# Keys and values of two heads on alternate partitions, and a new order of VectorE's steps, in a decode kernel fed from memory

## The chip, the cores and the metric

The kernel runs on one core of a Trainium2 chip. A core has a matrix engine (TensorE, in the profile PE, and PEld for its weight loads), a vector engine (VectorE, DVE), a scalar engine (ScalarE, ACT), GpSimd (POOL) and a queue engine that issues most loads (SyncE, SP). Sixteen DMA engines move data between the chip's memory (HBM) and the core's buffer (SBUF); TensorE writes into PSUM.

The metric is the device time of one execution in microseconds (us). Before the change the median of three runs is 128.31 us (128.28 to 128.5).

## The reference

Two branches read the same normalized row of 576 numbers, and both are added to it. Branch A is attention of one query over the last 4096 keys of a cache, with 32 query heads and 16 key heads, so that two query heads share a key head. Branch B is a gated MLP with a spatial gate, which for a sequence of length one is a scale and a shift.

```python
def _A_ref(x, k_cache, v_cache, wq, wo):
    W = min(4096, max(256, Sk // 4))          # 4096 of 65536
    q = (x @ wq).reshape(B, Sq, 32, 128)
    k = repeat(k_cache[:, :, Sk - W:, :], 2)   # 16 key heads for 32 query heads
    v = repeat(v_cache[:, :, Sk - W:, :], 2)
    scores = einsum('bhqd,bhkd->bhqk', q, k) * 128 ** (-0.5)
    p = softmax(scores)
    return einsum('bhqk,bhkd->bhqd', p, v).reshape(B, Sq, 4096) @ wo

def _B_ref(x, w_in, w_sp, b_sp, w_out):
    z = gelu(x @ w_in)                         # 4608 wide
    z1, z2 = z[..., :2304], layernorm(z[..., 2304:])
    g = w_sp * z2 + b_sp                       # one number each
    return (z1 * g) @ w_out

xn = layernorm(x)
return x + _A_ref(xn, ...) + _B_ref(xn, ...)
```

Weights, keys and values are bf16. Every byte of them is used once, and together they are 50.96 MB.

## The kernel before

**Loads.** All large loads go through one queue (SP), in the order in which lines 96 to 109 write them: `wq` in two parts, key pairs k0 and k1, `win` in three parts, then k2, v0, k3, v1 and so on to v7, then `wout` and `wo` in six parts (10, 8, 6, 4, 2 and 2 of its 32 rows a partition). They share a ring of seven slots of 20.7 KB a partition (`RING`). A load is issued when the transfer queue's turn comes and the slot that it takes has been given back by the last instruction that read it; SP waits in order, so a load that must wait holds up the ones after it.

**Keys and values.** One load brings two heads (`load_kv`, line 86). Each partition gets 32 consecutive positions of the first head (8 KB) and 32 of the second.

**Scores.** TensorE needs the 128 elements of a key along partitions. DVE transposes blocks of 32 by 32 words of four bytes (`t_head`, line 243: two instructions of 128x1024 a head); `s_head` (line 251) then multiplies with `Qb`, in which each query is laid out so that four accumulating matmuls per 512 positions give the scores of both query heads. The four heads of a group (GK) use four sets of 32 PSUM partitions of `S`; two such tiles alternate between groups.

**Softmax.** `sm_a` (line 275) takes the maximum over a partition's 1024 scores, spreads it over the partitions of a head with small transposes (`spread`, line 263) and lets ACT compute the exponential of the whole tile, with the sum. `sm_b` (line 286) transposes the result (`pt`, one instruction), spreads the sums the same way, takes the reciprocal, and lets ACT copy sixteen blocks of 32x32 words into `PT`.

**Product with the values.** `pv` (line 302) runs 128 matmuls into the one tile `ops`, 32 for each head of the group. `yb` (line 313) multiplies with the reciprocals and a mask (`om`), adds up (`on`), gathers with four small matmuls (`yps`) and copies to `Y`.

**MLP.** `z_mms` (line 330) multiplies with `win`; `z_rest` and `z_norm` (lines 340 and 363) are gelu, the second layernorm and the gate, in small steps on DVE with one exponential on ACT and one power on POOL.

**Order.** The order is written out by hand (line 70 turns the planner's own order off), and each engine works through its instructions in that order. The loop from line 381 runs over the 16 heads; `sm_a` of a group stands after the transposes of the first head of the next one, `sm_b` after those of the second, `yb` a group later, `pv` after the fourth. After the loop come the last group's softmax, `yb` of the third group, `pv`, two thirds of the product with `wout` (`out_hv`), `yb` of the last group, the rest of `wout` and the 64 matmuls with `wo`. These accumulate in two PSUM tiles; two copies and one store end the kernel.

Of the kernel before, what the change touches and what calls it, by code (L numbers as in the profile page):

```python
# [16 lines left out]
HKV = 16  # L17
DH = 128
# [2 lines left out]
F = 4608  # L21
FH = 2304
NT = W // 128
TB = 8
NB = NT // TB
GK = 4
NG = HKV // GK
NR = 98
NF = FH // 128
CW = D // 2  # L30
# [9 lines left out]
def kernel(  # L40
# [34 lines left out]
    def ring_tile(name, rows, width):  # L75
        t = ring.tile([P, SLOT], BF16, name=name, tag="ring")
        return t[:, 0:rows * width].rearrange("p (s c) -> p s c", c=width)
# [6 lines left out]
        return [(lo + s, v[:, s, :]) for s in range(n)]  # L84

    def load_kv(src, m, name):
        v = ring_tile(f"{name}{m}", 2, NT * DH)
        nc.sync.dma_start(v, src[0, 2 * m:2 * m + 2, SK - W:SK, :].rearrange("h (p t) d -> p h (t d)", p=P))
        return {2 * m + h: v[:, h, :].rearrange("p (t d) -> p t d", d=DH) for h in range(2)}

    def load_n(src, per, lo, n, name):
        v = ring_tile(f"{name}{lo}", n, D)
# [3 lines left out]
    K, V = {}, {}  # L96
    wq_sb = load_halves(A_wq, 0, 5, "wq") + load_halves(A_wq, 5, 4, "wq")
    for m in range(2):
        K.update(load_kv(A_k_cache, m, "k"))
    win_sb = sum((load_halves(B_w_in, lo, 3, "win") for lo in (0, 3, 6)), [])  # L100
    for m in range(2, HKV // 2):
        K.update(load_kv(A_k_cache, m, "k"))
        V.update(load_kv(A_v_cache, m - 2, "v"))
    for m in range(HKV // 2 - 2, HKV // 2):
        V.update(load_kv(A_v_cache, m, "v"))
    wout_sb = load_n(B_w_out, NF, 0, NF, "wout")
    wo_sb = []
    for n in (10, 8, 6, 4, 2, 2):
# [34 lines left out]
    idv = ident[:].rearrange("p (i c h) -> p i c h", i=4, h=2)[:, :, 0:4, :]  # L143
    cm = const.tile([P, 4], FP32, name="cm")
    nc.vector.tensor_reduce(out=cm[:], in_=idv.rearrange("p i c h -> p c i h"), op=ALU.add,
                            axis=mybir.AxisListType.XY)
    dmask = const.tile([P, 4, DH], FP32, name="dmask")
    nc.gpsimd.tensor_copy(dmask[:], cm[:].unsqueeze(2).to_broadcast([P, 4, DH]))
    ihm = const.tile([P, 4, 2], FP32, name="ihm")
    nc.vector.reduce_sum(ihm[:], idv.rearrange("p i c h -> p i h c"), axis=AXX)  # L150

    sel = const.tile([P, 4, 32], FP32, name="sel")
    nc.gpsimd.memset(sel[:], 0.0)
    selv = sel[:].rearrange("p q (i h e) -> p q i h e", i=4, h=2)
    for dq in range(4):
        nc.gpsimd.tensor_copy(selv[:, dq, :, :, dq], ihm[:])
    S = []
    for n in range(2):
        t = ps_s.tile([P, 2, 512], FP32, name=f"S{n}")
# [4 lines left out]

    mx = lead.tile([P, 32], FP32, name="mx")
    nc.gpsimd.memset(mx[:], 0.0)
    lx = const.tile([P, 32], FP32, name="lx")
    nc.gpsimd.memset(lx[:], 1.0)
    mb = const.tile([P, 32], FP32, name="mb")
    nc.gpsimd.memset(mb[:], 0.0)  # L170
    lb = const.tile([P, 32], FP32, name="lb")
    nc.gpsimd.memset(lb[:], 1.0)


    nc.tensor.matmul(ps_x[:, 0:NS], lhsT=rmat[:], rhs=x64[:], start=True, stop=True)  # L175
# [64 lines left out]
    KT = {}  # L240
    st = {}

    def t_head(j):
        kT = ktpool.tile([P, NT, 2, 32, 2], BF16, name=f"kT{j}", tag="kT")
        src = K[j].rearrange("p t d -> p (t d)").bitcast(FP32)
        dst = kT[:].rearrange("p t b k e -> p (t b k e)").bitcast(FP32)
        for hf in range(2):
            nc.vector.transpose(dst[:, 1024 * hf:1024 * (hf + 1)], src[:, 1024 * hf:1024 * (hf + 1)])  # L248
        KT[j] = kT

    def s_head(j):
        g, i = divmod(j, GK)
        kv = KT.pop(j)[:].rearrange("p t b k e -> p b e t k")
        for hf in range(2):
            for be in range(4):
                nc.tensor.matmul(  # L256
                    S[g % 2][32 * i:32 * i + 8, hf, :],
                    lhsT=Qb[:, j, be].rearrange("p a h -> p (a h)"),
                    rhs=kv[:, be // 2, be % 2, 16 * hf:16 * hf + 16, :],
                    start=(be == 0), stop=(be == 3), tile_position=(0, 32 * i),  # L260
                )

# [12 lines left out]
    def sm_a(g):  # L275
        s = S[g % 2]
        nc.vector.tensor_reduce(out=mx[:, 0:1], in_=s[:], op=ALU.max, axis=mybir.AxisListType.XY)  # L277
        bk = spread(mx, mb, g, ALU.max, "m")
        nm = work.tile([P, 1], FP32, name=f"nm{g}", tag="nm")
        nc.vector.tensor_scalar_mul(nm[:], bk[:, 0:1], -SCALE)  # L280
        p = work.tile([P, 1024], BF16, name=f"p{g}", tag="p")
        nc.scalar.activation(p[:], s[:].rearrange("p a n -> p (a n)"), ACT.Exp, bias=nm[:, 0:1], scale=SCALE,  # L282
                             accum_out=lx[:, 0:1])
        st[g] = {"p": p}

    def sm_b(g):
        d = st[g]
        pt = work.tile([P, NT, 32], BF16, name=f"pt{g}", tag="pt")
        nc.vector.transpose(pt[:].rearrange("p t x -> p (t x)"), d["p"][:])  # L289
        lbk = spread(lx, lb, g, ALU.add, "l")  # L290
        rs = work.tile([P, 1], FP32, name=f"rs{g}", tag="rs")
        nc.vector.reciprocal(rs[:], lbk[:, 0:1])
        PT = work.tile([P, GK, NT, 2], BF16, name=f"PT{g}", tag="PT")
        pt4 = pt[:].rearrange("p t x -> p (t x)").bitcast(FP32).rearrange("p (t x) -> p t x", x=16)
        PT4 = PT[:].rearrange("p i t h -> p (i t h)").bitcast(FP32).rearrange("p (i t) -> p i t", i=GK)
        for i in range(GK):
            for a in range(4):
                nc.scalar.copy(PT4[32 * a:32 * a + 32, i, :], pt4[32 * i:32 * i + 32, :, a])  # L298
        d["PT"] = PT
        d["rs"] = rs  # L300

    def pv(g):
        d = st[g]
        for tb in range(NT // 4):
            for i in range(GK):
                nc.tensor.matmul(  # L306
                    ops[32 * i:32 * i + 8, :],
                    lhsT=d["PT"][:, i, 4 * tb:4 * tb + 4, :].rearrange("p t h -> p (t h)"),
                    rhs=V[GK * g + i][:, 4 * tb:4 * tb + 4, :],
                    start=(tb == 0), stop=(tb == NT // 4 - 1), tile_position=(0, 32 * i),  # L310
                )

    def yb(g):
        d = st[g]
        om = work.tile([P, 4, DH], FP32, name=f"om{g}", tag="om")
        nc.vector.scalar_tensor_tensor(out=om[:].rearrange("p c d -> p (c d)"), in0=ops[:],  # L316
                                       scalar=d["rs"][:, 0:1], in1=dmask[:].rearrange("p c d -> p (c d)"),
                                       op0=ALU.mult, op1=ALU.mult)
        on = work.tile([P, DH], FP32, name=f"on{g}", tag="on")
        nc.vector.reduce_sum(on[:], om[:].rearrange("p c d -> p d c"), axis=AXX)  # L320
        yps = ps_m.tile([P, 32], FP32, name=f"yps{g}", tag="m")
        for dq in range(4):
            nc.tensor.matmul(  # L323
                yps[32 * g:32 * g + 32, :], lhsT=sel[:, dq, :], rhs=on[:, 32 * dq:32 * dq + 32],
                start=(dq == 0), stop=(dq == 3), tile_position=(0, 32 * g),
            )
        nc.vector.tensor_copy(Y[32 * g:32 * g + 32, :], yps[32 * g:32 * g + 32, :])


    def z_mms():  # L330
# [6 lines left out]
                                 skip_group_check=True)  # L337
        return zps

    def z_rest(zps):  # L340
# [6 lines left out]
        nc.vector.tensor_mul(u[:], u[:], z[:])  # L347
        th = const.tile([P, 2, NF], FP32, name="th")
        nc.scalar.activation(th[:], u[:], ACT.Exp, scale=-2.0 * GELU_C)
        nc.vector.tensor_scalar_add(th[:], th[:], 1.0)  # L350
        nc.vector.reciprocal(th[:], th[:])
        G = const.tile([P, 2, NF], FP32, name="G")
# [25 lines left out]
        nc.vector.tensor_mul(hv[:], G[:, 0], zn[:])  # L378
        return hv

    for j in range(HKV):
        t_head(j)
        g, o = divmod(j, GK)
        if g > 0 and o == 0:
            sm_a(g - 1)
        if g > 0 and o == 1:
            sm_b(g - 1)
        s_head(j)
        if j == GK - 1:
            zps = z_mms()  # L390
        if j == GK + 1:
            G, sz = z_rest(zps)

            acc = []
            for n, pool in enumerate((ps_a, ps_b)):
                t = pool.tile([P, 512], FP32, name=f"acc{n}", tag="ab"[n])
                acc.append(t[32 * n:32 * n + 1, 0:CW])
                nc.tensor.matmul(acc[n], lhsT=ones_b[:, 0:1], rhs=xrow[:, CW * n:CW * (n + 1)],
                                 start=True, stop=False, tile_position=(0, 32 * n))
        if j == GK + 2:  # L400
            hv = z_norm(G, sz)
        if g > 1 and o == 0:
            yb(g - 2)
        if g > 0 and o == 3:
            pv(g - 1)

    def out_mms(lhs, col, wv, last):
        for n in range(2):
# [15 lines left out]
    out_hv(2)  # L424
    for t, wv in wo_sb:
        out_mms(Y, t, wv, t == 31)
# [35 lines left out]
```

## Time and profile before

| | |
|---|---|
| median of 3 runs | 128.31 us (128.28 to 128.5) |
| profiled execution | 128.45 us, its span 126.6 us |
| PE, PEld | 76.2 and 33.7 us busy (60% and 27%) |
| DVE | 74.0 us busy (58%), 155 instructions |
| ACT, POOL | 23.3 and 3.6 us busy |
| read from HBM | 50.96 MB, 403 GB/s over the span |
| key transposes on DVE | 32 of 1213 ns |
| score matmuls on PE | 128, 43.4 us busy |
| exponentials on ACT | 4 of 1113 ns |
| copies to `PT` on ACT | 64 of 241 ns |
| granted TensorE clock, mean | 0.771 |

The profile is one execution. The span goes from its first to its last instruction; the other 1.85 us of the execution's time lie around it. The page cuts the span into 40 slices of 3.2 us and gives for each how busy an engine was, in tenths, and what the DMA engines moved. Groups of instructions are named by line, engine, operation and tile (`kT<-k`), with the number of partitions by elements. The chain follows back from the last instruction to what released each step. "Idle before" is time in which an engine waited just before an instruction, with what ended the wait. Busy times of matmuls overlap, since TensorE runs them in a pipeline and on several column groups at a time.

### The profile page before, as it was taken

To read this page: it belongs to the slowest core of one execution; us is meant where nothing else is said; L and a number is where in the kernel's file an instruction comes from. 1 tells how busy PE (TensorE), PEld (TensorE's weight loads), DVE (VectorE), ACT (ScalarE), POOL (GpSimd) and SP (SyncE) were. 2 spreads that over 40 slices of the span, in tenths; PEclk is the share of its full clock that TensorE was granted. 3 is DMA by queue.
4 is the path that set the end of the run, shared out by engine and by line. 5 is a ranking of instruction groups with operands and counts; after the bars stand their busy time and mean duration, and the time that the engine had idled before them with its cause. 6 is when DMAs were issued, how large, how long until landed. Compare 5 with 4: busy or idle time off the path is not lost.

```text
span 126.6 us, 1582 instructions
## 1 busy us (share of the span) xinstructions
PE 76.2 (60%) x610; PEld 33.7 (27%) x610; DVE 74.0 (58%) x155; ACT 23.3 (18%) x77; POOL 3.6 (3%) x19
## 2 busy tenths in 40 slices
PE   0002831399999797508449555993579920798461
PEld 0001301132699721102113121331113300345230
DVE  6704135999100499454299889998899359123001
ACT  1200011000000003930000306503065037500001
POOL 3401000000000000000100000000000000000000
PEclk9999998559995555875556995599655798559999
DMA  4999999999999999999999999999999999999950
GB/s 136 447 402 425 407 432 427 440 433 441 419 411 427 422 422 430 427 427 427 430 427 430 427 427 425 425 430 422 430 430 422 432 460 443 405 412 422 412 219 0
DMA packets 6174, 51.04 MB, mean 403 GB/s; under 512 B 534, under 2 KB 536, under 8 KB 1048
## 3 DMA queue, kind: packets, MB, share of 16 engines
q1 hardware_dynamic: 6082, 50.96, 95.5%
q8 instruction: 4, 0.07, 0.2%
q10 hardware_dynamic: 86, 0.00, 0.0%
q14 instruction: 2, 0.02, 0.0%
HBM read 50.96 MB, written 0.00 MB: 403 GB/s over the span
## 4 chain that ended last, share of the span: by engine, by line
issue 41%; DVE 25%; DMA 15%; PE 12%; ACT 4%; POOLq 0%; POOL 0%; ACTq 0%
DVE kT L248 11%; DMA wo<-in_A_wo_dram 8%; PE S L256 7%; DMA x<-in_A_x_dram 7%; ACT PT L298 3%; PE ops L306 3%; DVE mx L277 3%; DVE pt L289 3%; DVE on L320 2%; DVE om L316 1%; ACT p L282 1%; PE yps L323 1%; DVE mt L266 1%; DVE mb L272 1%; PE ps_x L185 0%
## 5 line engine op out<-in xcount | busy, mean ns | idle before, releaser
L256 PE MATMUL S<-kT,Qb 128*8 128x512 bf16 x128 | 43.4, 532 | 19.6 <-DVE kT L248 19.2
L248 DVE STREAM_TRANSPOSE kT<-k 128x1024 f32<-128x1024 f32 x32 | 37.0, 1213 | 10.7 <-DMA k<-in_A_k_cache_dram 10.6
L256 PEld LDWEIGHTS <-Qb 128*8 128x8 bf16 x128 | 12.5, 104 | 45.6 <-issue 39.2
L298 ACT COPY PT<-pt 32x32 f32<-32x32 f32 x64 | 15.4, 241 | 13.5 <-DVE pt L289 12.7
L282 ACT ACTIVATE p<-S,nm 128x1024 bf16<-128x1024 f32 x4 | 4.5, 1113 | 55.5 <-DVE nm L280 55.5
L306 PE MATMUL ops<-v,PT 128*8 128x512 bf16 x128 | 14.3, 478 | 0.4 <-ACT PT L298 0.4
L335 PEld LDWEIGHTS <-win 128*128 128x128 bf16 x162 | 10.1, 163 | 0.4 <-issue 0.4
L335 PE MATMUL zps<-XT,win 128*128 128x2 bf16 x162 | 10.2, 202 | 0.0
L323 PE MATMUL yps<-on,sel 128*32 128x32 f32 x32 | 1.9, 209 | 9.6 <-DVE on L320 9.6
L409 PE MATMUL acc<-wo,Y 128*1 128x288 bf16 x64 | 4.9, 285 | 3.2 <-DMA wo<-in_A_wo_dram 3.0
L277 DVE TENSOR_REDUCE mx<-S 128x1 f32<-128x1024 f32 x4 | 4.8, 1205 | 2.4 <-PE S L256 2.4
L175 PE MATMUL ps_x<-x,rmat 64*128 64x9 bf16 x1 | 0.2, 163 | 9.4 <-DMA x<-in_A_x_dram 9.4
L306 PEld LDWEIGHTS <-PT 128*8 128x8 bf16 x128 | 4.1, 91 | 6.3 <-issue 3.0
L289 DVE STREAM_TRANSPOSE pt<-p 128x1024 bf16<-128x1024 bf16 x4 | 4.8, 1210 | 1.4 <-ACT p L282 1.4
L316 DVE SCALAR_TENSOR_TENSOR om<-ops,rs,dmask 128x512 f32<-128x512 f32 x4 | 3.0, 742 | 4.2 <-PE ops L306 4.2
L429 DVE CAST res<-acc 1x288 bf16<-1x288 f32 x1 | 0.4, 446 | 8.5 <-PE acc L409 8.5
L323 PEld LDWEIGHTS yps<-on,sel 128*32 128x32 f32 x32 | 1.5, 122 | 11.5 <-DVE on L320 9.6
L208 PE MATMUL qps<-wq,XT 128*2 128x512 bf16 x36 | 4.0, 627 | 0.8 <-DVE XT L199 0.8
L320 DVE TENSOR_REDUCE on<-om 128x128 f32<-128x512 f32 x4 | 4.1, 1026 | 0.1
L409 PEld LDWEIGHTS <-Y 128*1 128x1 bf16 x64 | 2.8, 82 | 5.3 <-issue 4.4
L219 DVE CAST q_rep<-qps 128x512 bf16<-128x512 f32 x2 | 1.4, 692 | 4.6 <-PE qps L208 3.9
L217 ACT CAST q_rep<-qps 128x512 bf16<-128x512 f32 x2 | 1.2, 586 | 14.6 <-DVE q_rep L219 14.6
(89 smaller groups left out, 37.7 us busy)
## 6 DMA issues: line engine op xcount, KB each, us to landing
k<-in_A_k_cache_dram SPq DMA_DIRECT2D x8, 2048.0 KB, 23.3
v<-in_A_v_cache_dram SPq DMA_DIRECT2D x8, 2048.0 KB, 20.7
win<-in_B_w_in_dram SPq DMA_DIRECT2D x3, 1728.0 KB, 22.4
wout<-in_B_w_out_dram SPq DMA_DIRECT2D x1, 2592.0 KB, 26.6
wq<-in_A_wq_dram SPq DMA_DIRECT2D x1, 2560.0 KB, 8.7
wq<-in_A_wq_dram SPq DMA_DIRECT2D x1, 2048.0 KB, 12.9
wo<-in_A_wo_dram SPq DMA_DIRECT2D x1, 1440.0 KB
wo<-in_A_wo_dram SPq DMA_DIRECT2D x1, 1152.0 KB
```

Source lines behind the costliest of these rows:

```text
L248: nc.vector.transpose(dst[:, 1024 * hf:1024 * (hf + 1)], src[:, 1024 * hf:1024 * (hf + 1)])
L256: nc.tensor.matmul(S[g % 2][32 * i:32 * i + 8, hf, :], lhsT=Qb[:, j, be].rearrange("p a h -> p (a h)"), rhs=kv[:, be // 2, be % 2, 16 * hf ...
L277: nc.vector.tensor_reduce(out=mx[:, 0:1], in_=s[:], op=ALU.max, axis=mybir.AxisListType.XY)
L282: nc.scalar.activation(p[:], s[:].rearrange("p a n -> p (a n)"), ACT.Exp, bias=nm[:, 0:1], scale=SCALE, accum_out=lx[:, 0:1])
L289: nc.vector.transpose(pt[:].rearrange("p t x -> p (t x)"), d["p"][:])
L298: nc.scalar.copy(PT4[32 * a:32 * a + 32, i, :], pt4[32 * i:32 * i + 32, :, a])
L306: nc.tensor.matmul(ops[32 * i:32 * i + 8, :], lhsT=d["PT"][:, i, 4 * tb:4 * tb + 4, :].rearrange("p t h -> p (t h)"), rhs=V[GK * g + i][:, ...
L316: nc.vector.scalar_tensor_tensor(out=om[:].rearrange("p c d -> p (c d)"), in0=ops[:], scalar=d["rs"][:, 0:1], in1=dmask[:].rearrange("p c ...
L320: nc.vector.reduce_sum(on[:], om[:].rearrange("p c d -> p d c"), axis=AXX)
L323: nc.tensor.matmul(yps[32 * g:32 * g + 32, :], lhsT=sel[:, dq, :], rhs=on[:, 32 * dq:32 * dq + 32], start=(dq == 0), stop=(dq == 3), tile_ ...
L335: nc.tensor.matmul(zps[:, :, t], lhsT=wt[:, t, :], rhs=XT[:, s, :], start=(s == 0 and t == 0), stop=(s == NS - 1 and t == NF - 1), skip_gr ...
L409: nc.tensor.matmul(acc[n], lhsT=lhs[:, col:col + 1], rhs=wv[:, CW * n:CW * (n + 1)], start=False, stop=last, tile_position=(0, 32 * n))
```

## The change

1. **Layout of keys and values.** A load still brings two heads, but partition 2r + h now holds 64 consecutive positions of head h: one run of 16 KB instead of two of 8 KB. The loads, their order, their sizes and the ring stay.
2. **Transposes and scores.** The same 32 transposes are now made by halves of a pair (`t_half`), not by heads. After a transpose the columns of the two heads alternate, so `s_half` reads every other pair of elements: the matmul's moving operand steps by 8 bytes, where it stepped by 4. A half gives 512 scores of each of two heads, four accumulating matmuls in one set of 32 PSUM partitions and four in another.
3. **Softmax.** The exponential becomes two instructions of 64 partitions, each writing every other element of a tile twice as large (`pz`, two buffers, zero elsewhere, set at the start by POOL). `pt` takes two transposes instead of one, the sixteen copies to `PT` have 64 words a row instead of 32, and a `pv` matmul has 16 weight columns instead of 8. The sums go into a column of `lx` and are spread by one matmul with a constant 0/1 matrix (`lsum`, made at the start), read by a maximum with 0.5 and a reciprocal (`recip`), in place of `spread`.
4. **Order.** `sm_a` of a group stands at the end of its own group, ahead of the next pair's transposes; `sm_b` of the first group follows at once, of later ones after the second half of the next group. The exponential of gelu, its rest and the norm run together after the pair k2. `yb` is cut into `norm`, `y_mms` and `y_copy`; `norm` stands between the transposes of a group's last half and the maximum. At the end, `norm` of the third group and its four matmuls stand ahead of `sm_b` of the last group.

```diff
     def load_kv(src, m, name):
-        v = ring_tile(f"{name}{m}", 2, NT * DH)
-        nc.sync.dma_start(v, src[0, 2 * m:2 * m + 2, SK - W:SK, :].rearrange("h (p t) d -> p h (t d)", p=P))
-        return {2 * m + h: v[:, h, :].rearrange("p (t d) -> p t d", d=DH) for h in range(2)}
+        t = ring.tile([P, SLOT], BF16, name=f"{name}{m}", tag="ring")
+        v = t[:, 0:TP * DH]
+        nc.sync.dma_start(v, src[0, 2 * m:2 * m + 2, SK - W:SK, :].rearrange("h (r t) d -> r h (t d)", t=TP))
+        return v.rearrange("p (t d) -> p t d", d=DH)
...
+    lsum = const.tile([P, 4, 8, 2, 2], FP32, name="lsum")
+    nc.gpsimd.memset(lsum[:], 0.0)
+    for hd in range(2):
+        for pr in range(2):
+            for th in range(2):
+                nc.gpsimd.tensor_copy(lsum[:, 2 * pr + th, 0:4, hd, :],
+                                      oha[:, 2 * hd + pr, :].unsqueeze(1).to_broadcast([P, 4, 2]))
+    pz = []
+    for n in range(2):
+        t = const.tile([P, TP, 16, 2], BF16, name=f"pz{n}")
+        nc.gpsimd.memset(t[:], 0.0)
+        pz.append(t)
...
+    def t_half(m, hf):
+        kT = ktpool.tile([P, NT, 2, 16, 2, 2], BF16, name=f"kT{m}_{hf}", tag="kT")
+        src = K[m][:, NT * hf:NT * (hf + 1), :].rearrange("p t d -> p (t d)").bitcast(FP32)
+        dst = kT[:].rearrange("p t b r x e -> p (t b r x e)").bitcast(FP32)
+        for n in range(2):
+            nc.vector.transpose(dst[:, 1024 * n:1024 * (n + 1)], src[:, 1024 * n:1024 * (n + 1)])
+        KT[m, hf] = kT
+
+    def s_half(m, hf):
+        g, pr = divmod(m, 2)
+        kv = KT.pop((m, hf))[:].rearrange("p t b r x e -> p b e x t r")
+        for hd in range(2):
+            i = 2 * hd + pr
             for be in range(4):
                 nc.tensor.matmul(
                     S[g % 2][32 * i:32 * i + 8, hf, :],
-                    lhsT=Qb[:, j, be].rearrange("p a h -> p (a h)"),
-                    rhs=kv[:, be // 2, be % 2, 16 * hf:16 * hf + 16, :],
+                    lhsT=Qb[:, 2 * m + hd, be].rearrange("p a h -> p (a h)"),
+                    rhs=kv[:, be // 2, be % 2, hd],
                     start=(be == 0), stop=(be == 3), tile_position=(0, 32 * i),
                 )
...
-        p = work.tile([P, 1024], BF16, name=f"p{g}", tag="p")
-        nc.scalar.activation(p[:], s[:].rearrange("p a n -> p (a n)"), ACT.Exp, bias=nm[:, 0:1], scale=SCALE,
-                             accum_out=lx[:, 0:1])
+        p = pz[g % 2]
+        for hd in range(2):
+            lo, hi = 64 * hd, 64 * hd + 64
+            nc.scalar.activation(p[lo:hi, :, :, hd], s[lo:hi].rearrange("p a (t r) -> p (a t) r", r=16), ACT.Exp,
+                                 bias=nm[lo:hi, 0:1], scale=SCALE, accum_out=lx[lo:hi, g:g + 1])
...
+        for n in range(2):
+            nc.vector.transpose(dst[:, 1024 * n:1024 * (n + 1)], src[:, 1024 * n:1024 * (n + 1)])
...
+    def sums(g):
+        lps = ps_m.tile([P, 32], FP32, name=f"lps{g}", tag="m")
+        nc.tensor.matmul(lps[:, 0:1], lhsT=lsum[:].rearrange("p q c x h -> p (q c x h)"), rhs=lx[:, g:g + 1],
+                         start=True, stop=True)
+        st[g]["lps"] = lps
+
+    def recip(g):
+        rs = work.tile([P, 1], FP32, name=f"rs{g}", tag="rs")
+        nc.vector.tensor_scalar_max(rs[:], st[g]["lps"][:, 0:1], 0.5)
+        nc.vector.reciprocal(rs[:], rs[:])
+        st[g]["rs"] = rs
...
+    for j in range(2 * NP):
         g, o = divmod(j, GK)
+        t_half(j // 2, j % 2)
+        if o == 3:
+            if g > 0:
+                recip(g - 1)
+            if g > 1:
+                norm(g - 2)
+        s_half(j // 2, j % 2)
         if g > 0 and o == 1:
+            if g > 1:
+                sm_b(g - 1)
+            else:
+                G, sz = z_gelu(*z_exp(zps))
+                ...
+                hv = z_norm(G, sz)
+        if g > 0 and o == 2:
+            sums(g - 1)
+        if o == 3:
+            if g > 1:
+                y_mms(g - 2)
+            sm_a(g)
+            if g > 1:
+                y_copy(g - 2)
+            if g > 0:
+                pv(g - 1)
+            else:
+                zps = z_mms()
+                sm_b(0)
...
     g = NG - 1
-    sm_a(g)
+    norm(g - 1)
+    y_mms(g - 1)
     sm_b(g)
-    yb(g - 1)
+    y_copy(g - 1)
+    sums(g)
     pv(g)
+    recip(g)
     out_hv(0)
     out_hv(1)
-    yb(g)
+    norm(g)
+    y_mms(g)
+    y_copy(g)
     out_hv(2)
```

More of the change, by code (lines that the diff above doesn't have):

```diff
@@ L23 @@
 NT = W // 128
-TB = 8
-NB = NT // TB
 GK = 4
 NG = HKV // GK
+NP = HKV // 2
+TP = 2 * NT
 NR = 98
@@ L98 @@
     for m in range(2):
-        K.update(load_kv(A_k_cache, m, "k"))
+        K[m] = load_kv(A_k_cache, m, "k")
     win_sb = sum((load_halves(B_w_in, lo, 3, "win") for lo in (0, 3, 6)), [])
[L101 to L105, printed above, removed]
+    for m in range(2, NP):
+        K[m] = load_kv(A_k_cache, m, "k")
+        V[m - 2] = load_kv(A_v_cache, m - 2, "v")
+    for m in range(NP - 2, NP):
+        V[m] = load_kv(A_v_cache, m, "v")
     wout_sb = load_n(B_w_out, NF, 0, NF, "wout")
@@ L141 @@
     nc.vector.reduce_sum(mask4[:], ident[:].rearrange("p (a x) -> p a x", a=4), axis=AXX)
-    idv = ident[:].rearrange("p (i c h) -> p i c h", i=4, h=2)[:, :, 0:4, :]
+    idv = ident[:].rearrange("p (q c hh) -> p q c hh", q=4, hh=4)[:, :, 0:4, :]
     cm = const.tile([P, 4], FP32, name="cm")
-    nc.vector.tensor_reduce(out=cm[:], in_=idv.rearrange("p i c h -> p c i h"), op=ALU.add,
+    nc.vector.tensor_reduce(out=cm[:], in_=idv.rearrange("p q c hh -> p c q hh"), op=ALU.add,
                             axis=mybir.AxisListType.XY)
@@ L148 @@
     nc.gpsimd.tensor_copy(dmask[:], cm[:].unsqueeze(2).to_broadcast([P, 4, DH]))
-    ihm = const.tile([P, 4, 2], FP32, name="ihm")
-    nc.vector.reduce_sum(ihm[:], idv.rearrange("p i c h -> p i h c"), axis=AXX)
+    ohm = const.tile([P, 2, 4], FP32, name="ohm")
+    for pr in range(2):
+        nc.vector.tensor_reduce(out=ohm[:, pr, :], in_=idv[:, 2 * pr:2 * pr + 2].rearrange("p q c hh -> p hh q c"),
+                                op=ALU.add, axis=mybir.AxisListType.XY)
     sel = const.tile([P, 4, 32], FP32, name="sel")
     nc.gpsimd.memset(sel[:], 0.0)
-    selv = sel[:].rearrange("p q (i h e) -> p q i h e", i=4, h=2)
+    selv = sel[:].rearrange("p q (r hh e) -> p q r hh e", r=2, hh=4)
     for dq in range(4):
-        nc.gpsimd.tensor_copy(selv[:, dq, :, :, dq], ihm[:])
+        nc.gpsimd.tensor_copy(selv[:, dq, :, :, dq], ohm[:])
+    ids = ident[:].rearrange("p (i a h) -> p i a h", i=4, h=2)[:, :, 0:4, :]
+    oha = const.tile([P, 4, 2], FP32, name="oha")
+    nc.vector.reduce_sum(oha[:], ids.rearrange("p i a h -> p i h a"), axis=AXX)
+    lsum = const.tile([P, 4, 8, 2, 2], FP32, name="lsum")
+    nc.gpsimd.memset(lsum[:], 0.0)
+    for hd in range(2):
+        for pr in range(2):
+            for th in range(2):
[6 more added lines that the diff above has]
+        pz.append(t)
     S = []
@@ L166 @@
     nc.gpsimd.memset(mx[:], 0.0)
-    lx = const.tile([P, 32], FP32, name="lx")
-    nc.gpsimd.memset(lx[:], 1.0)
+    lx = const.tile([P, NG], FP32, name="lx")
     mb = const.tile([P, 32], FP32, name="mb")
     nc.gpsimd.memset(mb[:], 0.0)
-    lb = const.tile([P, 32], FP32, name="lb")
-    nc.gpsimd.memset(lb[:], 1.0)
     nc.tensor.matmul(ps_x[:, 0:NS], lhsT=rmat[:], rhs=x64[:], start=True, stop=True)
@@ L241 @@
     st = {}
[L243 to L254, printed above, removed]
+    def t_half(m, hf):
[10 more added lines that the diff above has]
+            i = 2 * hd + pr
             for be in range(4):
@@ L287, in sm_b @@
         d = st[g]
[L288 to L293, printed above, removed]
+        pt = work.tile([P, TP, 32], BF16, name=f"pt{g}", tag="pt")
+        src = d["p"][:].rearrange("p t r x -> p (t r x)")
+        dst = pt[:].rearrange("p t x -> p (t x)")
+        for n in range(2):
+            nc.vector.transpose(dst[:, 1024 * n:1024 * (n + 1)], src[:, 1024 * n:1024 * (n + 1)])
+        PT = work.tile([P, 2, TP, 2, 2], BF16, name=f"PT{g}", tag="PT")
         pt4 = pt[:].rearrange("p t x -> p (t x)").bitcast(FP32).rearrange("p (t x) -> p t x", x=16)
-        PT4 = PT[:].rearrange("p i t h -> p (i t h)").bitcast(FP32).rearrange("p (i t) -> p i t", i=GK)
+        PT4 = PT[:].rearrange("p r t x h -> p (r t x h)").bitcast(FP32).rearrange("p (r t x) -> p r x t", r=2, x=2)
         for i in range(GK):
             for a in range(4):
-                nc.scalar.copy(PT4[32 * a:32 * a + 32, i, :], pt4[32 * i:32 * i + 32, :, a])
+                nc.scalar.copy(PT4[32 * a:32 * a + 32, i % 2, i // 2, :], pt4[32 * i:32 * i + 32, :, a])
         d["PT"] = PT
-        d["rs"] = rs
+    def sums(g):
[8 more added lines that the diff above has]
+        st[g]["rs"] = rs
     def pv(g):
@@ L304, in pv, with norm @@
         for tb in range(NT // 4):
-            for i in range(GK):
+            for q in range(4):
+                pr, t0 = q // 2, NT * (q % 2) + 4 * tb
                 nc.tensor.matmul(
[L307 to L310, printed above, removed]
+                    ops[32 * q:32 * q + 16, :],
+                    lhsT=d["PT"][:, pr, t0:t0 + 4].rearrange("p t x h -> p (t x h)"),
+                    rhs=V[2 * g + pr][:, t0:t0 + 4, :],
+                    start=(tb == 0), stop=(tb == NT // 4 - 1), tile_position=(0, 32 * q),
                 )
-    def yb(g):
+    def norm(g):
         d = st[g]
@@ L320, in yb, with y_mms @@
         nc.vector.reduce_sum(on[:], om[:].rearrange("p c d -> p d c"), axis=AXX)
+        d["on"] = on
+    def y_mms(g):
+        d = st[g]
         yps = ps_m.tile([P, 32], FP32, name=f"yps{g}", tag="m")
@@ L323, in yb, with y_copy @@
             nc.tensor.matmul(
-                yps[32 * g:32 * g + 32, :], lhsT=sel[:, dq, :], rhs=on[:, 32 * dq:32 * dq + 32],
+                yps[32 * g:32 * g + 32, :], lhsT=sel[:, dq, :], rhs=d["on"][:, 32 * dq:32 * dq + 32],
                 start=(dq == 0), stop=(dq == 3), tile_position=(0, 32 * g),
             )
-        nc.vector.tensor_copy(Y[32 * g:32 * g + 32, :], yps[32 * g:32 * g + 32, :])
+        d["yps"] = yps
+    def y_copy(g):
+        nc.vector.tensor_copy(Y[32 * g:32 * g + 32, :], st[g]["yps"][32 * g:32 * g + 32, :])
     def z_mms():
@@ L338, in z_mms, with z_exp @@
         return zps
-    def z_rest(zps):
+    def z_exp(zps):
         z = const.tile([P, 2, NF], FP32, name="z")
@@ L349, in z_rest, with z_gelu @@
         nc.scalar.activation(th[:], u[:], ACT.Exp, scale=-2.0 * GELU_C)
+        return z, th
+    def z_gelu(z, th):
         nc.vector.tensor_scalar_add(th[:], th[:], 1.0)
@@ L379, in z_norm @@
         return hv
-    for j in range(HKV):
-        t_head(j)
+    for j in range(2 * NP):
         g, o = divmod(j, GK)
-        if g > 0 and o == 0:
-            sm_a(g - 1)
-        if g > 0 and o == 1:
[L387 to L405, printed above, removed]
+        t_half(j // 2, j % 2)
[5 more added lines that the diff above has]
+        s_half(j // 2, j % 2)
+        if g > 0 and o == 1:
+            if g > 1:
+                sm_b(g - 1)
+            else:
+                G, sz = z_gelu(*z_exp(zps))
+                acc = []
+                for n, pool in enumerate((ps_a, ps_b)):
+                    t = pool.tile([P, 512], FP32, name=f"acc{n}", tag="ab"[n])
+                    acc.append(t[32 * n:32 * n + 1, 0:CW])
+                    nc.tensor.matmul(acc[n], lhsT=ones_b[:, 0:1], rhs=xrow[:, CW * n:CW * (n + 1)],
+                                     start=True, stop=False, tile_position=(0, 32 * n))
+                hv = z_norm(G, sz)
[12 more added lines that the diff above has]
+                sm_b(0)
     def out_mms(lhs, col, wv, last):
```

## The prediction

> **What bounds the kernel now.** I read the page's slices and queue table first, then the chain that ended last, then windows and the timeline of the end. A measurement of this kernel tells about 0.2% (0.26 us) from no change.
>
> Page, slices and queues:
>
> ```profile
> DMA  4999999999999999999999999999999999999950
> GB/s 136 447 402 425 407 432 427 440 433 441 419 411 427 422 422 430 427 427 427 430 427 430 427 427 425 425 430 422 430 430 422 432 460 443 405 412 422 412 219 0
> ...
> q1 hardware_dynamic: 6082, 50.96, 95.5%
> ```
>
> The loads occupy the 16 DMA engines from the second slice to the thirty-eighth without a gap. PE and DVE are busy 60% and 58%. So what counts is how fast 50.96 MB stream in, and what remains after the last byte.
>
> The chain in order of time, its end:
>
> ```profile
> 112.91 0.03 issue
> 112.94 10.55 DMA wo<-in_A_wo_dram
> 123.49 0.04 issue
> 123.53 0.45 PE acc L409 x4
> 123.98 0.43 DVE res L429
> ```
>
> The last `wo` load ends it: four matmuls, the copy and the store follow. The chain also names DVE and PE in earlier steps, but only because the last `wo` issues wait for `pv(3)` to free their slots; those two issues (112.5 and 112.9) land 10.3 to 10.6 us later, so they stood in a queue.
>
> Timeline of the end, PE and DVE:
>
> ```profile
> 112.94 0.75 DVE L316 SCALAR_TENSOR_TENSOR om<-ops,rs,dmask 128x512 f32<-128x512 f32 x1 [4.21 <-PE ops L306]
> 113.72 1.04 DVE L320 TENSOR_REDUCE on<-om 128x128 f32<-128x512 f32 x1
> ...
> 115.29 0.20 DVE L327 CAST Y<-yps 32x32 bf16<-32x32 f32 x1 [0.53 <-PE yps L323]
> ...
> 115.98 1.39 PE L409 MATMUL acc<-wo,Y 128*1 128x288 bf16 x20
> ...
> 118.72 1.15 PE L409 MATMUL acc<-wo,Y 128*1 128x288 bf16 x16 [1.35 <-DMA wo<-in_A_wo_dram]
> ...
> 120.78 0.90 PE L409 MATMUL acc<-wo,Y 128*1 128x288 bf16 x12 [0.92 <-DMA wo<-in_A_wo_dram]
> ```
>
> `Y` is ready at 115.49, and from then PE waits for `wo` four times, 3.0 us in all. That is how much the attention may be late before it shows.
>
> **Part 1: 16 KB runs.** Windows of the trace (the last column is GB/s):
>
> ```profile
> 28.00:35.00 7.00, 6.70 (x51) 3.31 (x50) 4.11 (x4) 0.00 (x0) 0.00 (x0) 1.00 1.01 431
> ...
> 64.00:76.00 12.00, 8.13 (x61) 2.78 (x62) 10.92 (x16) 1.21 (x2) 0.00 (x0) 0.78 1.01 428
> ```
>
> The first window moves mostly `win` (6912 elements, 13.8 KB a run), the second only keys and values (8 KB a run). Both keep all engines busy, so the difference is a cost per run. At 428 GB/s, 8192 B on one of 16 engines take 16 x 8192 / 428 = 306.2 ns; at 431, 13824 B take 513.2 ns. The 5632 B between them cost 207.0 ns, 37.6 ns per 1024 B, which leaves 306.2 - 8 x 37.6 = 5 ns for every run. A 16 KB run pays that once instead of twice. Each engine gets 16 transfers x 128 / 16 = 128 such runs: 128 x 5 ns = 0.64 us. I take 0.6; ends 0 (the rates are rounded, and the two windows move different tensors) and 0.9 (427.5 against 431.5, the widest that rounding allows: 7 ns a run).
>
> Source order changes too: each partition now reads one head, the next the other head, 16 MB away. The present load reads both heads from each partition at the same distance and reaches 428. [...]
>
> **Part 2: setup.** POOL gets two memsets of 128x2048 and nine small steps for `lsum`. Its rows 128x32 (124 ns) and 128x128 (199 ns) give 0.78 ns an element: 1.65 us each, 3.3 together; `lsum` 0.2 + 8 x 0.14 = 1.3; two old memsets go. POOL sat idle 7.06 us before `mv`, so 2.4 us of cover remain. DVE's two more reductions (0.16 each) lie in 3.96 us of idle time. If the cover were gone, the first transposes would move, ahead of 10.64 us of idle time before k2. Cost 0.
>
> **Part 3: the loop.** DVE gains a second `pt` transpose per group (+1.20 each) and loses `spread` of the sums (four rows, 0.71); a maximum and a reciprocal (0.32) replace one reciprocal. All groups: about +2.6 us on an engine idle 42% of the span. `sm_a(0)` and `sm_b(0)` move to before k2: S of group 0 ends near 33.2, then 2.3 (maximum to `nm`), 2.4 (exp twice), 2.4 (`pt` twice) end at 40.3, inside the idle time to 42.75. The k2 transposes then run unbroken and z follows, with ACT free (2.67 us of waiting for it goes); k3 is released near 60 instead of 66.0. The DMA issues on SP keep their order. Later K releases, too, follow landings: k7 was issued at 70.84 and landed 20.7 us later, of which one transfer is 4.9; some 15 us of queued loads cover a late release. Cost 0; without the cover each us of lateness beyond it costs a us.
>
> On PE a half now puts four matmuls into one group of PSUM rows and four into another. Eight of one group took 3.57 us at clock 0.5; `pv`, with four groups side by side, ran 128 in about 3.6. So a half takes 1.8 (side by side) to 3.57 (one after the other). But a half needs both its transposes, where a head could start after the first. Old S of k7, 16 matmuls, ran 94.79 to 100.24.
>
> **Part 4: the end of the attention.** This is where cover is thin, so I follow it with the order of the changed DVE queue.
>
> - k7 lands at 91.5, 0.5 earlier by part 1. DVE is then finishing `pt(2)` (k6 transposes after 81.5 to 83, `pt` to 91.6 at the latest). Four transposes (4.6) end at 96.2, `recip(2)` and `norm(1)` at 98.3.
> - S of the last half: 96.2 + 1.8 = 98.0 side by side, 99.4 at the old rate (5.45 for 16 from 93.9). So `mx` starts at 98.3 to 99.4, against 100.26 before.
> - From `mx` to `Y` took 115.49 - 100.26 = 15.23. Added: a second exp, nearest row 1.11 + 0.19 of which 1.2 is on the path (ends 1.2 and 2.4, if the strided output halves its speed); a second `pt`, 1.2; 16 copies of 64 instead of 32 elements, by ACT's rows 128x36 (233 ns) and 128x1024 (1113) 0.89 ns an element, so 16 x 28 ns = 0.5 (ends 0 and 3.9, twice the row). `norm(2)` now stands ahead of `pt(3)` and waits for `pv(2)`, which waits behind `y_mms(1)` for `norm(1)`: `pv(2)` 98.7 to 102.3, `norm(2)` to 104.1, exp done at 103.2, so +0.9. `pt(3)`, the Y copy and the ACT copies are queued behind it. `sums(3)` waits on PE for that Y copy, but PE waits for `PT` anyway. Sum 15.23 + 3.8 = 19.0.
> - `Y` at 117.3 to 118.4, that is 1.8 to 2.9 us later than before.
> - Without waits, 64 `wo` matmuls take 1.39 + 44 x 0.061 = 4.1 (slope from the x20 and x12 rows), starting 0.5 after `Y`: PE ends at 121.9 to 123.0. The loads let it end at 123.94 - 0.6 = 123.3. Hidden, by 0.3 to 1.4 us.
> - `pv(3)` ends near 115 instead of 112.9; the last `wo` issues stood 10.3 us in the queue and need some 2 to 3 of it. Cost 0.
>
> Sum: -0.6 on the profiled 128.45 (span 126.6 and 1.85 around it) is 127.85; the profile lies 0.14 above the median 128.31, so **127.7**.
>
> **Rivals.**
>
> 1. *The attention's end takes over.* For: cover of 0.3 to 1.4 us against additions of 3.8, with prices from other shapes. Against: `mx` starts earlier. It decides once `Y` is later than 118.7, and makes the kernel slower than before once `Y` is later than 119.4 (119.4 + 0.5 + 4.1 = 124.0). With the copies at their upper end (+3.4) `Y` is at 120.7 to 121.8, PE ends 1.4 to 2.5 later than now: 129.7 to 130.8; halfway, 128.0 to 129.0.
> 2. *Nothing gained.* Runs of 8 KB already saturate, and 3 GB/s between windows is what rounding and other tensors make: 128.3.
> 3. *The stream slows*, because alternate heads from partition to partition meet worse in memory. No row shows that. One per cent on 78 us is 0.8 us: 129.1.
> 4. *S slows*: keys are now read in steps of 8 bytes instead of 4. Twice the S time at the end adds 3.6: `Y` near 121.5, so 130.5. Against: the present 4 byte step costs nothing that shows; at full clock these matmuls start 0.22 us apart (82.96, 83.19, 83.41), as the `pv` ones do, which read without a step.
>
> **How the numbers follow.** Forecast with the end hidden 0.57, of which 0.05 are gains beyond 0.6 (127.1 to 127.4); rival 2 0.14; rival 1 0.17 (0.02 of it still faster, 0.02 within 0.2%, as the gain of part 1 pays for a little lateness); rivals 3 and 4 0.12 together. Faster 0.57 + 0.02 = 0.59, same 0.14 + 0.02 = 0.16, slower 0.13 + 0.12 = 0.25. The forecast's own range is 127.4 to 128.0. The stated range reaches to rival 1's halfway case and one per cent of rival 3: 127.2 to 129.3.
>
> **What the changed profile would show.** Right: 431 GB/s in windows of keys and values alone; about 4030 packets on q1 instead of 6082; DVE busy between 33 and 42 us; k3's last transpose near 60; `Y` at 117 to 118.5; PE still waiting for `wo` before its last four matmuls. Wrong: matmuls on `wo` without waits (rival 1), a window still at 428 or below (2, 3), S halves of 7 us at clock 0.5 (4), or a slice of DMA under 9, meaning a release came too late.

## The result and the profile after

The changed kernel takes 127.67 us (median of 6 runs, 127.52 to 127.76), the kernel before, run beside it, 128.38 (128.26 to 128.55). The ratio is 0.9943, with a 95% interval of 0.993 to 0.9956: faster by a little over half a per cent. The forecast was 127.7.

The page after, its slices and queues (compare with the lines shown of before):

```profile
span 125.9 us, 1614 instructions
...
DMA  4999999999999999999999999999999999999950
GB/s 130 417 427 437 432 422 442 419 426 433 435 429 427 442 416 416 437 437 432 437 422 432 437 427 432 432 416 437 437 424 437 427 426 453 409 416 415 419 226 0
...
q1 hardware_dynamic: 4034, 50.96, 95.3%
```

The span is 0.7 us shorter. The same bytes pass in 4034 packets instead of 6082, and no slice of DMA shows a gap, so no slot was given back too late. The stage that counts is the long stretch in which only keys and values pass. The windows of that stretch, before and then after (after the stretch and its length come the busy times of PE, PEld, DVE, ACT and POOL, then the granted clock, the share of the DMA engines' time and GB/s):

```profile
48.00:90.00 42.00, 25.49 (x148) 8.42 (x148) 33.11 (x64) 10.98 (x39) 0.55 (x1) 0.70 1.01 428
```

```profile
48.00:90.00 42.00, 22.65 (x150) 6.85 (x147) 32.04 (x52) 12.33 (x31) 0.55 (x1) 0.83 1.01 431
```

428 became 431. The rates are rounded; the completion records of the trace give more figures. The first of the 16 completions of k2 and that of v7, 13 loads later, lie 104.06 - 40.36 = 63.70 us apart before and 103.37 - 40.16 = 63.21 after: 4.900 and 4.862 us a load. Sixteen loads at 0.038 us make 0.61 us of the 0.71 us between the medians; the remaining 0.1 us is less than a measurement of this kernel can tell from nothing (0.26 us, as the prediction has it).

The end of the kernel after, from the timeline:

```profile
110.74 3.34 PE L344 MATMUL ops<-v,PT 128*16 128x512 bf16 x30 [0.64 <-ACT PT L321]
...
114.13 0.75 DVE L354 SCALAR_TENSOR_TENSOR om<-ops,rs,dmask 128x512 f32<-128x512 f32 x1 [7.11 <-PE ops L344]
114.92 1.03 DVE L358 TENSOR_REDUCE on<-om 128x128 f32<-128x512 f32 x1
...
116.47 0.20 DVE L372 CAST Y<-yps 32x32 bf16<-32x32 f32 x1 [0.53 <-PE yps L365]
...
116.89 2.37 PE L467 MATMUL acc<-wo,Y 128*1 128x288 bf16 x36
120.12 0.90 PE L467 MATMUL acc<-wo,Y 128*1 128x288 bf16 x12 [0.87 <-DMA wo<-in_A_wo_dram]
...
121.50 1.10 PE L467 MATMUL acc<-wo,Y 128*1 128x288 bf16 x12 [0.48 <-DMA wo<-in_A_wo_dram]
...
122.87 0.41 PE L467 MATMUL acc<-wo,Y 128*1 128x288 bf16 x4 [0.28 <-DMA wo<-in_A_wo_dram]
```

`Y` comes 1.2 us later than before, at 116.47 instead of 115.29, and PE has to wait less often for `wo` (1.6 us in three waits, where it was 3.0 in four). But it still waits three times, up to the last four matmuls: the loads set the end, and those are 0.66 us earlier (122.87 against 123.53).

### The profile page after: what moved, and what is told of

It reads as the page before. It is cut to its first block, busy times and chain, and to the rows that moved or that the text cites. A ratio compares the mean times of both kernels' runs of the same rounds, so it can differ in the third digit from the quotient of the medians.

```text
span 125.9 us, 1614 instructions
## 1 busy us (share of the span) xinstructions
PE 67.8 (54%) x618; PEld 30.9 (25%) x618; DVE 77.3 (61%) x149; ACT 33.6 (27%) x85; POOL 8.2 (7%) x28
## 3 DMA queue, kind: packets, MB, share of 16 engines
q1 hardware_dynamic: 4034, 50.96, 95.3%
## 4 chain that ended last, share of the span: by engine, by line
DMA 56%; PE 16%; DVE 14%; ACT 7%; issue 3%; SPq 1%; POOL 0%; ACTq 0%
DMA k<-in_A_k_cache_dram 43%; DMA x<-in_A_x_dram 7%; DMA wo<-in_A_wo_dram 7%; DVE kT L268 6%; PE ops L344 6%; PE S L277 5%; ACT PT L321 4%; PE qps L227 3%; ACT pz L305 2%; DVE Qb L255 2%; DVE pt L315 2%; DVE q_rep L238 1%; ACT q_rep L236 1%; DVE on L358 1%; PE lps L327 1%
## 5 line engine op out<-in xcount | busy, mean ns | idle before, releaser
L277 PE MATMUL S<-kT,Qb 128*8 128x512 bf16 x128 | 32.5, 638 | 29.0 <-DVE kT L268 29.0
L305 ACT ACTIVATE pz<-S,nm 64x1024 bf16<-64x1024 f32 x8 | 11.3, 1409 | 45.1 <-DVE nm L301 30.4
L321 ACT COPY PT<-pt 32x64 f32<-32x64 f32 x64 | 18.9, 296 | 14.3 <-DVE pt L315 13.6
L277 PEld LDWEIGHTS <-Qb 128*8 128x8 bf16 x128 | 6.4, 96 | 48.4 <-issue 45.4
L344 PE MATMUL ops<-v,PT 128*16 128x512 bf16 x128 | 11.7, 451 | 3.5 <-ACT PT L321 3.5
L315 DVE STREAM_TRANSPOSE pt<-pz 128x1024 bf16<-128x1024 bf16 x8 | 9.4, 1214 | 4.2 <-ACT pz L305 4.2
L344 PEld LDWEIGHTS <-PT 128*16 128x16 bf16 x128 | 5.0, 98 | 7.4 <-ACT PT L321 4.1
L327 PE MATMUL lps<-lx,lsum 128*128 128x1 f32 x8 | 2.2, 343 | 3.2 <-DVE Y L372 3.2
```

Of the source, the lines that this page charges most:

```text
L277: nc.tensor.matmul(S[g % 2][32 * i:32 * i + 8, hf, :], lhsT=Qb[:, 2 * m + hd, be].rearrange("p a h -> p (a h)"), rhs=kv[:, be // 2, be % 2 ...
L305: nc.scalar.activation(p[lo:hi, :, :, hd], s[lo:hi].rearrange("p a (t r) -> p (a t) r", r=16), ACT.Exp, bias=nm[lo:hi, 0:1], scale=SCALE, ...
L315: nc.vector.transpose(dst[:, 1024 * n:1024 * (n + 1)], src[:, 1024 * n:1024 * (n + 1)])
L321: nc.scalar.copy(PT4[32 * a:32 * a + 32, i % 2, i // 2, :], pt4[32 * i:32 * i + 32, :, a])
L327: nc.tensor.matmul(lps[:, 0:1], lhsT=lsum[:].rearrange("p q c x h -> p (q c x h)"), rhs=lx[:, g:g + 1], start=True, stop=True)
L344: nc.tensor.matmul(ops[32 * q:32 * q + 16, :], lhsT=d["PT"][:, pr, t0:t0 + 4].rearrange("p t x h -> p (t x h)"), rhs=V[2 * g + pr][:, t0:t ...
```

## The experiments

Three theories were open. T: the gain comes from fewer runs, at some 5 ns each, and the new order only lies beside the loads. O: it comes from the new order. A: it comes from the order in which the two heads are read. The first three kernels cross them.

### Old order with long runs

```diff
-        v = ring_tile(f"{name}{m}", 2, NT * DH)
-        nc.sync.dma_start(v, src[...].rearrange("h (p t) d -> p h (t d)", p=P))
+        t = ring.tile([P, SLOT], BF16, name=f"{name}{m}", tag="ring")
+        f = t[:, 0:2 * NT * DH]
+        nc.sync.dma_start(f, src[...].rearrange("h (r t) d -> r h (t d)", t=2 * NT))
+        v = f.rearrange("p (s c) -> p s c", c=NT * DH)
```

> The kernel before with nothing changed but the loads of keys and values: one 16 KB run a partition, heads on alternate partitions. The compute is the old one, so it takes the two halves of a partition for two heads, and the attention's numbers are not the reference's; every instruction and every byte stays. Theory T (each run costs its DMA engine some 5 ns, the stream sets the end, the new order only lies beside it): 0.64 us less than before, 127.7 us, ratio 0.995; keys and values pass at 4.86 us a transfer instead of 4.90. Theory O (the new order, with slots given back earlier, brings the gain): 128.3, ratio 1.000. Theory A (not the length of a run but the order in which the two heads are read brings it): as T here.

127.74 us, ratio 0.9961 (0.9939 to 0.9983). The loads alone bring the gain, in the old order of the work. Its window:

```profile
48.00:90.00 42.00, 23.53 (x148) 8.11 (x148) 33.32 (x65) 10.75 (x39) 0.55 (x1) 0.78 1.01 432
```

k2 to v7 take 63.21 us, 4.862 a load, the pace of the changed kernel to the last digit.

### New order with runs of 8 KB

```diff
-        nc.sync.dma_start(v, src[...].rearrange("h (r t) d -> r h (t d)", t=TP))
+        w = v.rearrange("p (h e) -> p h e", h=2)
+        nc.sync.dma_start(w, src[...].rearrange("h (p t) d -> p h (t d)", p=P))
```

> The changed kernel with the old load: two runs of 8 KB a partition, both heads on every partition. The compute is the new one, so positions and heads are mixed and the attention's numbers are not the reference's; instructions and bytes stay. T: the gain is gone, 128.3 us, ratio 1.000, 4.90 us a transfer. O: the gain stays, 127.7, ratio 0.995. A: as T.

128.34 us, ratio 0.9985 (0.9963 to 1.0006). The gain is gone, while the whole new order, its halves, its second transposes and its longer exponential are there. The window:

```profile
48.00:90.00 42.00, 22.49 (x150) 6.82 (x147) 32.02 (x52) 11.69 (x29) 0.55 (x1) 0.80 1.01 428
```

4.900 us a load again. O falls: by itself the new order neither gains nor costs what can be measured.

### New order with runs of 4 KB

```diff
-        nc.sync.dma_start(v, src[...].rearrange("h (r t) d -> r h (t d)", t=TP))
+        w = v.rearrange("p (h e) -> p h e", h=4)
+        lo = min(2 * m, HKV - 4)
+        nc.sync.dma_start(w, src[0, lo:lo + 4, SK - W:SK - W // 2, :].rearrange("h (p t) d -> p h (t d)", p=P))
```

> The changed kernel with four runs of 4 KB a partition, from four heads and half the positions: the same number of bytes, but other keys and values, so the attention's numbers are not the reference's. T: 512 runs for each DMA engine instead of 128, 384 x 5 ns = 1.9 us more than the changed kernel: 129.6 us, ratio 1.010, 4.98 us a transfer. A: runs of 4 KB behave as those of 8 KB: 128.3, ratio 1.000. O: 127.7, ratio 0.995.

129.65 us, ratio 1.0096 (1.0072 to 1.0121). The window:

```profile
48.00:90.00 42.00, 23.31 (x152) 6.98 (x149) 32.23 (x53) 11.05 (x27) 0.55 (x1) 0.81 1.02 421
```

k2 to v7 take 105.49 - 40.82 = 64.67 us, 4.975 a load. An engine has 8, 16 or 32 runs in a load: from 16 KB to 8 KB a load grows by 0.038 us, 4.7 ns a run; from 8 KB to 4 KB by 0.075 us, again 4.7 ns a run. A cost per run fits three lengths, and it holds whether a partition reads one head, two or four. The trace of the kernel before has a fourth length, with no heads in it: the three `win` loads, one run of 13.8 KB a partition, follow each other every 4.109 us (their first completions lie at 27.24, 31.35 and 35.46). From the pace of the 16 KB loads and 4.7 ns a run one would expect 4.108. So A has no part left to explain.

### The end of the attention, 1.2 us later

```diff
                 nc.scalar.copy(PT4[32 * a:32 * a + 32, i % 2, i // 2, :], pt4[32 * i:32 * i + 32, :, a])
+        if g == NG - 1:
+            for n in range(4):
+                i, a = divmod(n, 4)
+                nc.scalar.copy(PT4[32 * a:32 * a + 32, i % 2, i // 2, :], pt4[32 * i:32 * i + 32, :, a])
```

> The changed kernel with four of the sixteen ACT copies of the last group made twice, 4 x 0.306 = 1.2 us on the chain that ends in Y. In the changed kernel 64 products with wo could end, without waits, near 121.0 (36 took 2.37 from 116.89, 28 more at 0.064), and the loads let them end at 123.3: a cover of 2.2 us. Theory cover: Y moves from 116.5 to 117.7, and the time stays 127.7, ratio 0.994 to 0.995. Rival (the end of the attention already shares the bound): 128.9, ratio 1.004.

127.70 us, ratio 0.9944 (0.9922 to 0.9965): no change from the changed kernel. The end of its timeline:

```profile
117.89 0.20 DVE L376 CAST Y<-yps 32x32 bf16<-32x32 f32 x1 [0.53 <-PE yps L369]
118.30 4.27 PE L471 MATMUL acc<-wo,Y 128*1 128x288 bf16 x60
122.84 0.41 PE L471 MATMUL acc<-wo,Y 128*1 128x288 bf16 x4 [0.27 <-DMA wo<-in_A_wo_dram]
```

`Y` came 1.4 us later than in the changed kernel (117.89 against 116.47), and the last four matmuls began at the same time (122.84 against 122.87). PE waited for `wo` once, 0.3 us, in place of three times and 1.6 us. The lateness was taken out of those waits. The time by which `Y` may be late before the end moves is what the expectations call the cover.

### The end of the attention, 4.9 us later

The same edit with `range(16)`.

> The changed kernel with all sixteen ACT copies of the last group made twice, 16 x 0.306 = 4.9 us on the chain that ends in Y. The run with four copies twice left PE one wait of 0.3 us for wo, so the cover is nearly used up at 1.2 us of lateness. Theory cover: PE then ends 4.9 - 2.2 = 2.7 us later than in the changed kernel, with no wait for wo: 130.4 us, ratio 1.016. Rival (PE catches up, because without waits it stays at a high clock and the four column groups fill): 129.0 or less.

130.81 us, ratio 1.0165 (1.0102 to 1.0228). The end of its timeline:

```profile
122.14 0.20 DVE L376 CAST Y<-yps 32x32 bf16<-32x32 f32 x1 [0.53 <-PE yps L369]
122.55 4.09 PE L471 MATMUL acc<-wo,Y 128*1 128x288 bf16 x64
126.67 0.45 DVE L496 CAST res<-acc 1x288 bf16<-1x288 f32 x1 [4.33 <-PE acc L471]
```

`Y` at 122.14, and all 64 matmuls in one row of 4.09 us with no wait for a load: here the attention sets the end, 3.35 us later than in the changed kernel (126.67 against 123.32), where cover predicted 2.7. `Y` came 5.7 us later, not 4.9: the copies took 0.32 each instead of 0.306, and `pv(3)` 3.58 against 3.34. From the end of `Y` to the end of PE went 122.34 to 126.64, 4.3 us. So in the changed kernel, whose PE ends at 123.28, `Y` could have been finished at 119.0 instead of 116.67: a cover of 2.3 us. The waits for `wo` on PE, 1.6 us, were less than that.

### Scores read in steps of 4 bytes

```diff
-        kv = KT.pop((m, hf))[:].rearrange("p t b r x e -> p b e x t r")
+        kv = KT.pop((m, hf))[:].rearrange("p t b r x e -> p t b (r x) e").rearrange("p t b (x r) e -> p b e x t r", x=2)
```

> The changed kernel with the score matmuls reading the same tile in steps of 4 bytes, as the kernel before did, in two blocks of sixteen: the columns of two heads are exchanged, so the scores are not the reference's. In the changed kernel the weight loads of a half's pairs follow each other every 0.47 us at clock 0.5, in the kernel before every 0.427. Theory step (8 byte steps slow the read): 0.427 here. Rival (two streams side by side, or something else): 0.47 stays. The time is 127.7 in both cases, since the scores lie beside the loads.

127.71 us in one run, no other time. Its profile says more than the expectation asked. A half of the changed kernel at full clock (1.00 in the window's third column from the end), first the window, then the timeline:

```profile
64.20:66.20 2.00, 1.96 (x8) 0.44 (x8) 2.00 (x2) 0.25 (x2) 0.00 (x0) 1.00 0.94 401
```

```profile
64.24 1.98 PE L277 MATMUL S<-kT,Qb 128*8 128x512 bf16 x8 [3.36 <-DVE kT L268]
```

and one of the kernel with steps of 4 bytes, also at full clock, window and timeline:

```profile
83.80:84.80 1.00, 0.92 (x8) 0.38 (x8) 1.00 (x2) 0.00 (x0) 0.00 (x0) 1.00 1.08 459
```

```profile
83.88 1.04 PE L277 MATMUL S<-kT,Qb 128*8 128x512 bf16 x8 [3.10 <-DVE kT L268]
```

With 8 byte steps eight matmuls take 1.98 us even at full clock, with 4 byte steps 1.04. At half clock (0.50 in the windows around them) it is 2.06 against 1.88, first the changed kernel, then the one with 4 byte steps, and 3.57 in the kernel before, whose eight matmuls stay in one set of PSUM partitions:

```profile
54.56 2.06 PE L277 MATMUL S<-kT,Qb 128*8 128x512 bf16 x8 [4.85 <-DVE kT L268]
```

```profile
54.63 1.88 PE L277 MATMUL S<-kT,Qb 128*8 128x512 bf16 x8 [4.66 <-DVE kT L268]
```

```profile
44.05 3.57 PE L256 MATMUL S<-kT,Qb 128*8 128x512 bf16 x8 [0.71 <-DVE kT L248]
```

The two matmuls of a pair, one for each head, start 0.013 us apart. So the step does slow the read, to a pace of about 0.46 us a pair that the clock hardly changes; at half clock, where a pair takes 0.43 with 4 byte steps, little of it shows. Whether one matmul alone would be slowed as much was not run. The kernel hardly pays for it, because two matmuls of different column groups run side by side and the scores lie beside the loads.

### A shorter program for TensorE

```diff
-            for t in range(NF):
+            for t in (range(NF) if s == 0 else [NF - 1]):
```

> The changed kernel with 27 of the 162 matmuls with win (all column blocks for the first ninth of the input, one for each other ninth): the MLP branch is not the reference's, all loads stay. PE's program is 270 instructions shorter. In the profiles a handful of code packets of 16 KB (queue q8) pass during the run, and the sixteen completions of one load lie 1.5 us apart at the end, where they lay 0.5 apart before the first such packet. Theory code: at least one packet fewer, and if it is that of an engine that ends last, up to 0.7 us less: 127.0 to 127.7, ratio 0.989 to 0.995. Rival (the spread has another cause): packets fewer, spread and time as in the changed kernel, 127.7.

127.79 us, ratio 0.9951 (0.9915 to 0.9987): not told apart from the changed kernel. The page counts three packets on the code queue instead of five, first the changed kernel, then this one:

```profile
q8 instruction: 5, 0.08, 0.2%
```

```profile
q8 instruction: 3, 0.05, 0.1%
```

The completions of the last load, taken from its own semaphore, still lie 1.7 us apart (121.08 to 122.74), where they lay 1.9 us apart in the changed kernel (120.95 to 122.83). The 1.5 us in the expectation is too small: consecutive loads overlap there, and it mixes their completions. Two code packets fewer did not move the end.

The traces do show where the spread comes from. Count, in each load, the DMA engines that complete more than 0.7 us after the first. There are none until a packet of the kind `instruction` passes (16 KB on q8, 8 KB on q14), and one more after each of those in the table:

| kernel | the first packets start at | late engines in the loads that land next |
|---|---|---|
| before | 36.20, 43.38, 46.46, 79.33 | 1, 2, 3, 4 |
| changed | 29.63, 36.33, 44.72, 77.98 | 1, 2, 3, 4 |
| shorter program | 29.42, 35.73, none near 44, 79.99 | 1, 2, still 2, 3 |

In the kernel before, fifteen engines complete k2 by 41.16, and one at 42.62 (by the semaphore, which steps some 0.35 us after the records used for the pace of the loads). In the changed kernel a 16 KB load packet that begins as one of the first three packets on q8 ends takes 1.09 to 1.16 us, where such packets take 0.61. An engine that is late stays late to the last load; only in the run above with `Y` 5.7 us later, which issued its last two loads at 119.37, does the last load end 0.45 us apart. So a code packet costs one engine up to some 1.5 us. The packet that this run lacks left one engine fewer late, but the end waits for the latest engine, and the other packets still made four late. In the changed kernel eleven engines have finished the last load by 121.65 and the last one by 122.83; that makes an estimate of 1.2 us for what the packets cost the end. No run is without them. The spread of the last load is the same before and after the change (1.84 and 1.88 us), so it has no part in the gain.

## Why the prediction was right

**Part 1** carried the sum, and it held by its own working. It took about 5 ns a run from two windows of different tensors and got 0.64 us. Measured: 4.7 ns a run, 0.61 us over 16 loads, shown by moving the run length alone in both directions. The upper end, 0.9, and the lower, 0, were both wider than needed. Heads that alternate from partition to partition, 16 MB apart, ran at 431 GB/s in the changed kernel and at 432 in the old order with long runs, as the 428 of the load before had suggested. Rivals 2 and 3 fall with it.

**Part 2** held closely. POOL's row for the two memsets is 3.55 us (forecast 3.3), and its idle time before `mv` 2.39 (forecast 2.4).

**Part 3.** DVE worked from 34.28 to 42.1, in the gap before k2, but its end lay 1.8 us later than the 40.3 forecast: the scores of the first group came 1.1 us later, and the exponentials were dearer (see part 4). Only 0.33 us of this gap were left. k3's last transpose ended at 56.8, not near 60: halves took 2.0 us, close to the side by side end, so the norm of the MLP waited 0.49 us for its matmul, where it had waited 3.06. The run with the new order and short runs shows that all of this is worth nothing by itself here.

**Part 4** came out with some terms off against each other. `mx` started at 97.99 (forecast 98.3 to 99.4). From there to the end of `Y` it took 18.7 us (forecast 19.0). Mis-sized were: the exponentials, where the strided output of 64 partitions takes 1409 ns against 1113 for 128 contiguous ones, so that the pair is 1.7 us longer and not 1.2; the copies, 296 ns on average for 64 elements, +0.8 with their gaps instead of +0.5; and `norm(2)`, which was to cost 0.9 and cost nothing, because `pv(2)` ran at full clock in 1.9 us and not in 3.6. The cover was forecast at 0.3 to 1.4 us and is 2.3: `Y` was complete at 116.67, 0.6 ahead of the earliest forecast, and what follows it takes 4.3 us and not 4.6. The opening remark, that the 3.0 us of waits for `wo` are how late the attention may be, is too low by the same measure: with 4.3 us from `Y` to the end of PE the kernel before had an estimated 123.94 - 4.3 - 115.49 = 4.1 us.

**Rival 1**, as a mechanism, is right and lies close: made late enough, the end takes over (130.81). Its point of decision, `Y` later than 118.7, is confirmed within 0.3 us by the 119.0 worked out above. Only the prices were not high enough.

**Rival 4** is where the prediction argued badly. It said that steps of 8 bytes would cost nothing because steps of 4 cost nothing. At full clock they halve the rate of the score matmuls, two of which run side by side (1.98 us for eight instead of 1.04). The doubled S time that it priced did not come, for a reason that stood in part 3: the two groups run side by side, so a half of 2.0 us replaces a head of up to 3.57.

## What to carry to other kernels

Here the loads filled the DMA engines from end to end, and each run cost its engine 4.7 ns. Where a trace shows the engines as full, count the runs of one engine, multiply by the difference that two windows with different run lengths show, and check that what the new layout adds elsewhere stays under the cover at the end. A reordering that gives slots back earlier was worth nothing here (128.34 us, ratio 0.9985), where the queue of loads never ran empty. The waits before the last matmuls show that there is cover, but not all of it (1.6 us against 2.3 here); a test that lengthens that chain on purpose finds its edge. And where the last load sets the end, look at its slowest DMA engine, not only at the mean rate: here it ended at 122.83, when eleven of the sixteen had finished by 121.65.

## What was not expected of the hardware

- Two matmuls side by side that read their moving operands in steps of 8 bytes (two bytes of every eight) keep a pace of about 0.46 us for 512 columns, at either clock; in steps of 4 bytes a pair takes 0.22 at full clock and 0.43 at half. Eight matmuls, in pairs, took 1.98 us instead of 1.04 at full clock, and 2.06 instead of 1.88 at half.
- Two accumulations into different sets of 32 PSUM partitions, issued one after the other (four, then four), run side by side. Eight matmuls of one half at half clock took 2.06 us (1.88 with steps of 4 bytes), eight of one head before, also in steps of 4 bytes, 3.57.
- The exponential takes longer for half the partitions when it writes every other element: 1409 ns for 64x1024 against 1113 for 128x1024 written without gaps. That the gaps are the cause is likely, but no run changes them alone.
- A packet of code that passes among the loads makes one DMA engine late, in the kernel before by about 1.5 us (42.62 against 41.16), and it stays late up to the last load, whose completions lie 1.84 us apart there.
